# Weight loads queued three chunks further ahead in a mixture-of-experts stage

## The chip, the cores and the metric

The kernel runs on one core of a Trainium2 chip. The time is device microseconds of one execution, from a launch of the whole program; the median of three runs of the kernel before is 403.86 us (402.92 to 403.9). TensorE (PE) does the products, VectorE (DVE) and ScalarE (ACT) the elementwise work, GpSimd (POOL) some more and the indirect transfers, and SyncE's queue (SP) issues most of the others.

## The reference

A retention layer (attention without a softmax, with a decay mask) over 8 batches, 8 heads, 576 positions and 64 channels a head gives x, 4608 tokens of 512 channels. Then comes a mixture of 8 experts with one expert for each token, all in float32:

```python
skip_score = x @ w_skip
do_compute = skip_score > 0            # other tokens pass unchanged
xc = x[do_compute]
logits = xc @ w_gate
e_idx = np.argmax(logits, axis=1)      # one expert of 8 for each token
gate_w = softmax(logits)[e_idx]
for e in range(8):
    h = np.maximum(xc[mask] @ w1[e], 0.0)          # 512 -> 1024
    y[mask] = gate_w[mask, None] * (h @ w2[e])     # 1024 -> 512
out[do_compute] = xc + y
```

## The kernel before, in words

The first part (to about 155 us) computes the retention layer in 36 groups of 128 tokens, writes x to DRAM and sorts the tokens into lists, one for each expert. The experts are ranked by their number of tokens and run from the fullest to the emptiest; here they are counted in that order, 0 to 7. Expert e has room for `CAPS[e]` tokens (368, 344, 332, 308, 304, 286, 278, 276): two full blocks of 128 and a rest.

Float32 is reached with two operands of a shorter format: a value is split into hi, which ACT casts, and lo, the difference, which DVE subtracts. A product is then three: hi with hi, hi with lo, lo with hi (`three`). PE runs these in an order written out by hand.

The 1024 hidden channels of an expert go in 8 chunks of 128. A step of the loop in `experts` is one chunk f of one expert e: `up` multiplies the tokens (xhi, xlo) with the first weights of the chunk into ph, 12 products; ACT makes hhi of it and DVE hlo; and `down`, which runs one step later, multiplies these with the second weights, 12 products again. So PE's order is up of this chunk, down of the one before, up of the next.

The weights of a chunk are one transfer of 512 KB (`load_w`, L158) into a staging tile w, of which there are 4 buffers. The split (`split_w`, L166 to L168) makes whi on ACT and wlo on DVE, each with 6 buffers. At a step, `experts` loads all chunks up to `AHEAD` = 5 ahead of this one and splits what it has loaded. The split of a chunk waits for `down` of the chunk six before it, whose buffer it takes.

The tokens of expert e are gathered from DRAM during expert e-1 (`gather_next`). From expert 2 on they are turned without PE: the rows go to DRAM (`hop_out`, the tile hop), come back in four pieces of 32 partitions (`hop_in`, the tile xh), and DVE transposes them (`turn_pieces`, the tile xt) and they are split into xhi (ACT) and xlo (DVE). There is one such pass for each of the two full blocks, in steps 4 and 5 of the expert before, and in step 6 one for the rests (`turn_pack`). Rests of several experts share a block; only experts 2 and 4 fetch one of their own (hop r, xh r, xt r), experts 3, 5 and 6 take their columns of one that is there already, and so does expert 7.

What sets the order: PE's is by hand. For the other engines a scheduler lays the instructions out when the program is built, by its own idea of the times, and the engines then keep that order. `hop_out` and `hop_in` say that their transfers are to be issued after the load that was asked for last (`marks["load"]`).

Of the kernel before, what the change touches and what calls it, by code (L numbers as in the profile page):

```python
# [48 lines left out]
UAHEAD = UBUFS - LAG  # L49
VBUFS = 3  # L50
AHEAD = 5
GROUPS = (8, 8, 8, 4, 4, 4)
KONE = 2
QD = 32
# [5 lines left out]
NCUT = 5  # L60
# [23 lines left out]
def kernel(  # L84
# [70 lines left out]
    def load_w(e, f, regs):  # L155

        t = wpool.tile([P, 2, NCC, P], F32, tag="w", name=f"w_{e}_{f}", bufs=4)
        marks["load"] = nc.sync.dma_start(t.rearrange("p m c i -> p (m c i)"), w[bass.ds(regs[e], 1), f].rearrange("o p c -> (o p) c"))  # L158
        return t
# [281 lines left out]
    def blocks(e):  # L441
        return [(k, min(P, CAPS[e] - k * P)) for k in range(NBLK)]
# [34 lines left out]
    with ExitStack() as actx:  # L477
# [254 lines left out]

        starts = np.cumsum((0,) + GROUPS).tolist()
        todo = []
        counted = []
        added = []
        chunks = []

        def weights():
# [4 lines left out]
            chunks.append(None)  # L744
            if 0 <= n - 2 < AHEAD:
                t = chunks[n - 2]
                hi, lo = wq[0, n - 2] = parts(t)
                tc.keep_in_program_order(nc.scalar.copy(hi, t))
                behind = ranked[-1] if len(ranked) == len(GROUPS) - 1 else None
                for m in range(2):  # L750
                    for c in range(0, NCC, NCC // 2):
# [3 lines left out]
                        if behind is not None:  # L755
# [6 lines left out]
                            behind = None  # L762
            if n < AHEAD:
                chunks[n] = load_w(0, n, regs)
# [19 lines left out]
        def route(b):  # L784
# [3 lines left out]
            k = starts.index((b + 1) * NB) - 1  # L788
            ra = route_a(starts[k], GROUPS[k])
            more = lambda: route_b(ps_m, k == 0, k > KCUT, k == KRANK, *ra)  # L790
# [67 lines left out]
        if LAG:  # L858
            stage_c(NT - 2)
        while len(chunks) < AHEAD + 2:  # L860
            weights()
# [199 lines left out]
    def experts(acts):  # L1061


        every = blocks(0)
        early, late = every[: CUT // P], every[CUT // P :]
        steps = [(0, f, early) for f in range(NCUT)] + [None] + [(0, f, late) for f in range(NCUT)]
        steps += [(0, f, every) for f in range(NCUT, NFC)]
        steps += [(e, f, blocks(e)) for e in range(1, NE) for f in range(NFC)]
        chunks = [(e, f) for e in range(NE) for f in range(NFC)]
        xg = {0: xg0}  # L1070
        xT = {0: (xhi0, xlo0)}
        begun = range(len(hs))
        py = {}
        last = None

        between = {}
        raw = {}

        def split_raw(most):
            for c in list(raw)[:most]:  # L1080
                wq[c] = split_w(raw.pop(c))

        def behind(mark, do, *args):
            with tc.issue_after(marks[mark].ins):
                do(*args)

        def at(e, f, place, do, *args):
            between.setdefault((e, f, place), []).append(lambda: do(*args))

        def turn_next(e):  # L1090
            xT[e] = [mp.tile([P, NCC, CAP], F32R, tag=x, name=f"{x}_{e}") for x in ("xhi", "xlo")]
            if e > 1:
                for k in range(NBLK):
                    at(e - 1, 4 + k, 0, lambda k=k: behind("up", turn_block, e, k, *xT[e]))
                return
            for c in range(NCC):
                where = ((5, 0), (6, 0), (6, 1), (7, 0))[c]
                at(e - 1, *where, lambda c=c: turn(e, xg[e], *xT[e], blocks(e)[:-1], [c], ("pt", "m")[c % 2]))
                if c == 1:
                    at(e - 1, *where, lambda: turn_pack(e, *xT[e], "pt"))  # L1100

        at(2, 7, 1, count_more)
        at(0, 6, 0, pack_move)
        at(0, 7, 1, lambda: behind("up", pack_ids))
        at(NE - 1, 4, 0, lambda: tc.keep_in_program_order(nc.gpsimd.drain()))
        for e in range(2, NE):
            at(e - 1, 0, 0, lambda e=e: gather_next(e, xg))
            hops = [(f"{e}_{k}", lambda e=e, k=k: xg[e][:, k, :]) for k in range(NBLK - 1)]
            if e == PACKS[PLACE[e][0]][0]:
                hops.append((f"r{PLACE[e][0]}", lambda e=e: xr[PLACE[e][0]]))  # L1110
            for k, (name, rows) in enumerate(hops):
                at(e - 1, 2 + k // 2, k % 2, lambda name=name, rows=rows: hop_out(name, rows()))
                at(e - 1, 3 + k // 2, k % 2, lambda name=name: hop_in(name))
        for n in range(len(steps) + 1):
            cur = steps[n] if n < len(steps) else None
            if n in acts:
                acts[n]()
            if cur:
                e, f, ks = cur
                i = chunks.index((e, f))  # L1120
                for c in chunks[i : i + AHEAD + 1]:
                    if c not in wq and c not in raw and c[0] < len(regs):
                        raw[c] = load_w(*c, regs)
                if ks is not late and n > 3:
                    split_raw(1 if i == NCUT else len(raw))
                if (e, f) not in hs:
                    tg, nb = (f"_{f}", 1) if e == 0 and f < NCUT else ("", 3)
                    hs[e, f] = [
                        mp.tile([P, CAP], F32R, tag=f"{x}{tg}", name=f"{x}_{e}_{f}", bufs=nb) for x in ("hhi", "hlo")
                    ]  # L1130
                if n not in begun:
                    tag = ("ph", "ph", "m", "pt", "py3")[f] if ks is late else "ph"
                    ph = bank(tag, f"ph_{e}_{f}_{ks[0][0]}", 2 if tag == "ph" else 1)
                    if ks is late:
                        up_late(f, ph, ks, wq[e, f], hs[e, f])
                    else:
                        up(ph, ks, xT[e], wq[e, f], hs[e, f])
                if (n, 1) in acts:
                    acts[n, 1]()
                    behind("lists", split_raw, 1)  # L1140
                    gather_next(1, xg)
                if f == 3 and ks is not early and e + 1 < NE:
                    turn_next(e + 1)
            place = cur and cur[2] is not early and cur[:2]
            for do in between.pop((*place, 0), ()) if place else ():
                do()
            if last and last[2] is late and cur[2] is late:
                last = None
            if last and last[2] is late:
                for f in range(NCUT):  # L1150
                    down(0, f, late, py[0], hs[0, f], wq[0, f])
                split_raw(len(raw))
            elif last:
                e, f, ks = last
                if e not in py:
                    py[e] = [bank(f"py{c}", f"py_{e}_{c}") for c in range(NBLK if e == 0 else NCC)]
                if n == NCUT:
                    down(e, f, ks[:1], py[e], hs[e, f], wq[e, f])
                    for cs, tag in (((0, 1), "pt"), ((2, 3), "py3")):
                        turn(0, xg0, xhi0, xlo0, late, cs, tag)  # L1160
                    ks = ks[1:]
                down(e, f, ks, py[e], hs[e, f], wq[e, f])
                if f == NFC - 1:
                    y = evacuate(e, py[e])
                    if e + 1 < NE:
                        ks = blocks(e)[:-1] if e else blocks(e)
                        for k, where in zip(ks, ((1, 1), (2, 0), (2, 1))):
                            at(e + 1, *where, finish, e, y, xg[e], [k])
                        if e and PACKS[PLACE[e][0]][-1] == e:
                            at(e + 1, 2, 1, finish_pack, PLACE[e][0])  # L1170
                    else:
                        finish(e, y, xg[e], blocks(e)[:-1], ("pt", "m"))
                        k, n = blocks(e)[-1]
                        finish_rest(yR[e], n, xr[PLACE[e][0]], gate[:, k, e : e + 1], sidx[:, k, e : e + 1], "ph")
            for do in between.pop((*place, 1), ()) if place else ():
                do()
            last = cur
        assert not between
# [16 lines left out]
    with tc.For_i(0, nblock, 1):  # L1195
# [7 lines left out]
        reg = expert_reg(mei[0:1, 0:1])  # L1203
        ws = [split_w(load_w(0, f, [reg])) for f in range(AHEAD)]
        ps2 = bank("m", "ps2")
# [3 lines left out]
        raw = rt.tile([P, NCMP], F32, tag="raw2", name="raw2")  # L1209
# [17 lines left out]
        for f in range(NFC):  # L1227
            if f + AHEAD < NFC:
                ws.append(split_w(load_w(0, f + AHEAD, [reg])))
# [81 lines left out]
```

## Time and profile before

| | |
|---|---|
| median of three runs | 403.86 us |
| the profiled execution | 407.06 us |
| its span, first to last instruction | 405.4 us |
| PE, DVE, ACT, POOL busy | 380.5, 279.8, 184.0, 154.1 us |
| DMA, mean over the span | 245 GB/s |
| mean granted clock of PE | 0.992 |

The profile is of one execution. Its time is longer than that of the runs without a profile. Busy time of PE is modelled at the ends of products, so a PE that is busy all the time is one whose products start one behind the other. The experts' stage is the part from about 165 us to 397.

### The profile page before, as it was taken

How to read it: one execution, taken by the hardware profiler on the slowest of the kernel's cores; microseconds unless marked ns; L12 is line 12 of the kernel's file. 1: busy time of each engine (PE TensorE's matmuls, PEld its weight loads, DVE VectorE, ACT ScalarE, POOL GpSimd, SP SyncE). 2: the span in 40 equal slices, each digit the busy share in tenths (PEclk: the TensorE clock that was granted, in tenths of full speed). 3: DMA queues.
4: the chain of work that ended last, by engine and by line, in shares of the span. 5: the costliest groups of instructions: out<-in, count | busy, mean ns of one | idle time of the engine just before them, and what ended most of it. 6: DMA issues, size and time to landing. Idle time of an engine off the chain costs nothing. (4 is left out here: it accounts for less than half of the span.)

```text
span 405.4 us, 12478 instructions
## 1 busy us (share of the span) xinstructions
PE 380.5 (94%) x4950; PEld 345.4 (85%) x4952; DVE 279.8 (69%) x623; ACT 184.0 (45%) x367; POOL 154.1 (38%) x210
## 2 busy tenths in 40 slices
PE   7899989989999887999999999999999999999992
PEld 3677777778787775979899999999999999999992
DVE  3665686588589788977756766797768567777512
ACT  2454544445444566115544543545535546455311
POOL 4965654565475489051032024023042032200402
PEclk9999999999999899999999999999999999999998
DMA  8998999999999986236987666776776776673101
GB/s 304 352 331 306 352 303 350 321 335 308 331 348 325 352 327 185 81 86 224 311 261 251 202 203 212 235 254 233 244 218 238 227 243 226 233 259 107 66 2 56
DMA packets 39420, 99.34 MB, mean 245 GB/s; under 512 B 5678, under 2 KB 12974, under 8 KB 39358
## 3 DMA queue, kind: packets, MB, share of 16 engines
q1 hardware_dynamic: 30366, 78.66, 57.5%
q0 software_dynamic: 3232, 9.99, 7.2%
q10 hardware_dynamic: 5760, 9.85, 6.5%
q8 instruction: 40, 0.66, 0.7%
q14 instruction: 22, 0.18, 0.1%
HBM read 80.63 MB, written 18.26 MB: 244 GB/s over the span
## 5 line engine op out<-in xcount | busy, mean ns | idle before, releaser
L168 DVE TENSOR_TENSOR wlo_w<-w,whi_w 128x1024 fp32r<-128x1024 f32 x59 | 71.9, 1224 | 38.3 <-ACT whi_w L167 37.7
L167 ACT CAST whi_w<-w 128x1024 fp32r<-128x1024 f32 x59 | 61.7, 1051 | 52.2 <-PE py L449 48.6
L981 POOL DMA_INDIRECT out<-rs,sidx x17 | 21.5, 1264 | 126.3 <-DVE rs L980 118.1
L449 PE MATMUL ph<-xhi,whi_w 128*128 128x344 f32 (+6 forms) x224 | 68.4, 305 | 0.0
L449 PE MATMUL py<-hhi,whi_w 128*128 128x344 f32 (+6 forms) x224 | 68.2, 304 | 0.0
L449 PE MATMUL py<-hhi,wlo_w 128*128 128x344 f32 (+6 forms) x224 | 67.7, 302 | 0.0
L449 PE MATMUL ph<-xlo,whi_w 128*128 128x344 f32 (+6 forms) x224 | 67.7, 302 | 0.0
L449 PE MATMUL ph<-xhi,wlo_w 128*128 128x344 f32 (+6 forms) x224 | 67.7, 302 | 0.0
L449 PE MATMUL py<-hlo,whi_w 128*128 128x344 f32 (+6 forms) x224 | 67.6, 302 | 0.0
L588 POOL TENSOR_TENSOR kn<-u,tt_sb 128x512 f32<-128x512 f32 x33 | 35.0, 1060 | 46.6 <-DMA u<-qkv 19.4
L457 ACT ACTIVATE hhi<-ph 128x344 fp32r<-128x344 f32 (+8 forms) x61 | 26.0, 426 | 57.3 <-PE ph L449 57.2
L580 ACT COPY u<-psc 64x256 f32<-64x256 f32 x64 | 23.4, 366 | 58.5 <-DVE u L576 52.5
L670 PE MATMUL pxt<-u,vs 128*64 128x128 f32 (+1 forms) x576 | 49.0, 273 | 0.1
L607 POOL TENSOR_TENSOR vs<-u,tt_sb 64x256 f32<-64x256 f32 x72 | 44.8, 622 | 9.5 <-PE pxt L670 4.4
L576 DVE TENSOR_TENSOR u<-psc,mt_sb 64x256 f32<-64x256 f32 x72 | 30.3, 420 | 23.5 <-PE pxt L646 10.5
L621 PEld LDWEIGHTS ps_s<-u,kn 128*64 128x64 f32 x512 | 31.8, 139 | 12.8 <-issue 5.9
L449 PEld LDWEIGHTS ph<-xhi,whi_w 128*128 128x128 f32 x224 | 42.2, 189 | 0.1
L449 PEld LDWEIGHTS ph<-xlo,whi_w 128*128 128x128 f32 x224 | 42.2, 188 | 0.1
L449 PEld LDWEIGHTS py<-hhi,whi_w 128*128 128x128 f32 x224 | 42.2, 189 | 0.0
L449 PEld LDWEIGHTS py<-hlo,whi_w 128*128 128x128 f32 x224 | 42.2, 188 | 0.0
L449 PEld LDWEIGHTS py<-hhi,wlo_w 128*128 128x128 f32 x224 | 42.2, 188 | 0.0
L449 PEld LDWEIGHTS ph<-xhi,wlo_w 128*128 128x128 f32 x224 | 42.2, 188 | 0.0
(216 smaller groups left out, 825.0 us busy)
## 6 DMA issues: line engine op xcount, KB each, us to landing
u<-qkv SPq DMA_DIRECT2D x72, 512.0 KB, 5.9
w<-w SPq DMA_DIRECT2D x64, 512.0 KB, 4.6
out<-xn ACTq DMA_DIRECT2D x36, 256.0 KB, 5.9
hop<-xg SPq DMA_DIRECT2D x12, 256.0 KB, 4.7
xh<-hop SPq DMA_DIRECT2D x48, 64.0 KB, 2.7
hop_r<-xr SPq DMA_DIRECT2D x2, 256.0 KB, 2.7
xh_r<-hop_r SPq DMA_DIRECT2D x8, 64.0 KB, 5.0
out<-rs,sidx POOLq DMA_INDIRECT x17, 5.8
```

Source lines behind the costliest of these rows:

```text
L167: nc.scalar.copy(hi, t)
L168: nc.vector.tensor_tensor(lo, t, hi.bitcast(F32), ALU.subtract)
L449: nc.tensor.matmul(ps, x, y, start=first and n == 0, stop=last and n == 3 * len(terms) - 1)
L457: nc.scalar.activation(hi, ph, AF.Relu)
L576: nc.vector.tensor_tensor(u_t[g][h, j, :, :D], near[h, :, :D], mt_sb[h].unsqueeze(1).broadcast_to([D, NPR, D]), ALU.mult)
L580: nc.scalar.copy(u_t[g][h, j, :, D:], near[h, :, D:])
L588: nc.gpsimd.tensor_tensor(kn_t[g].rearrange("p a (j i) -> p a j i", j=2), u_t[g][:, 3].rearrange("p a (j i) -> p a j i", j=2), tt_sb[:, k ...
L607: nc.gpsimd.tensor_tensor(vs_t[g][h, j], u_t[g][h, 2, :, j * D : (j + 1) * D], tt_sb[h, TV + g % NQ // 2, :].unsqueeze(2).broadcast_to([D, ...
L621: nc.tensor.matmul(ps_s[halves[j], i % 2, a, :], kn_t[g][:, a, j * D : (j + 1) * D], u_t[g][:, 2, a, j * D : (j + 1) * D], start=i == 0 an ...
L670: nc.tensor.matmul(pxt[halves[j], a, q], vs_t[g][:, j, a, :], u_t[g][:, j, a, q], start=False, stop=a == NPR - 1, skip_group_check=True,)
L981: done = nc.gpsimd.indirect_dma_start(out=out, out_offset=bass.IndirectOffsetOnAxis(ap=idx, axis=0), in_=rs[:n], in_offset=None, bounds_ch ...
```

## The change

A constant `LEAD` = 3 is added. From expert 1 on, a step asks for the loads of chunks up to 8 ahead instead of 5. What it splits are still the chunks up to 5 ahead: the others stay loaded and unsplit until their turn. The four staging buffers stay.

```diff
 AHEAD = 5
+LEAD = 3
...
-                for c in chunks[i : i + AHEAD + 1]:
+                for c in chunks[i : i + AHEAD + 1 + (LEAD if e else 0)]:
                     if c not in wq and c not in raw and c[0] < len(regs):
                         raw[c] = load_w(*c, regs)
+                due = sum(c in chunks[: i + AHEAD + 1] for c in raw)
                 if ks is not late and n > 3:
-                    split_raw(1 if i == NCUT else len(raw))
+                    split_raw(1 if i == NCUT else due)
```

No instruction is added or taken away. PE and GpSimd keep their order; SP, DVE and ACT get another one. On SP, where expert 2's rows are sent to DRAM and back, the rows before are these (w_7 is chunk 7 of expert 1, w_0 and w_1 are chunks of expert 2):

```order
L158 DMA w_7_3802<-w 128x1024
L1016 DMA hop_0_3825<-xg_3738 128x512
L1016 DMA hop_1_3844<-xg_3738 128x512
L354 TENSOR_LOAD order
L158 ISA
L158 DMA w_0_3851<-w 128x1024
L1022 DMA xh_0_3876<-hop_0_3825 32x4x128 x4
L1016 DMA hop_r_3881<-xr_3745 128x512
L1022 DMA xh_1_3895<-hop_1_3844 32x4x128 x4
L158 ISA
L158 DMA w_1_3900<-w 128x1024
L1022 DMA xh_r_3923<-hop_r_3881 32x4x128 x4
```

And now (w_2, w_3 and w_4 are all of expert 2; every line number is one higher):

```order
L159 DMA w_2_3808<-w 128x1024
L1017 DMA hop_0_3831<-xg_3744 128x512
L1017 DMA hop_1_3850<-xg_3744 128x512
L159 ISA
L159 DMA w_3_3857<-w 128x1024
L1023 DMA xh_0_3882<-hop_0_3831 32x4x128 x4
L1017 DMA hop_r_3887<-xr_3751 128x512
L1023 DMA xh_1_3901<-hop_1_3850 32x4x128 x4
L159 ISA
L159 DMA w_4_3906<-w 128x1024
L1023 DMA xh_r_3929<-hop_r_3887 32x4x128 x4
```

The hops and what fetches them back stand three loads further back, the order among them being the same.

On DVE at the end of expert 1, where expert 2's tokens are transposed, before (hlo_5 to hlo_7 are of expert 1, wlo_w_2 to wlo_w_4, xt and xlo of expert 2):

```order
L458 SCALAR_TENSOR_TENSOR hlo_5_3951<-ph_5_0_3952,hhi_5_3950 128x344
L1026 STREAM_TRANSPOSE xt_1_3967<-xh_1_3895 128x4x4x32
L168 TENSOR_TENSOR wlo_w_2_3944_3947<-w_2_3944,whi_w_2_3944_3946 128x1024
L173 TENSOR_TENSOR xlo_3875<-xt_1_3967,xhi_3874 128x4x128
L458 SCALAR_TENSOR_TENSOR hlo_6_3990<-ph_6_0_3991,hhi_6_3989 128x344
L1026 STREAM_TRANSPOSE xt_r_4006<-xh_r_3923 128x4x4x32
L168 TENSOR_TENSOR wlo_w_3_3983_3986<-w_3_3983,whi_w_3_3983_3985 128x1024
L173 TENSOR_TENSOR xlo_3875<-xt_r_4006,xhi_3874 128x4x76
L458 SCALAR_TENSOR_TENSOR hlo_7_4029<-ph_7_0_4030,hhi_7_4028 128x344
L168 TENSOR_TENSOR wlo_w_4_4022_4025<-w_4_4022,whi_w_4_4022_4024 128x1024
```

And now:

```order
L1027 STREAM_TRANSPOSE xt_1_3973<-xh_1_3901 128x4x4x32
L459 SCALAR_TENSOR_TENSOR hlo_6_3996<-ph_6_0_3997,hhi_6_3995 128x344
L174 TENSOR_TENSOR xlo_3881<-xt_1_3973,xhi_3880 128x4x128
L169 TENSOR_TENSOR wlo_w_3_3857_3992<-w_3_3857,whi_w_3_3857_3991 128x1024
L459 SCALAR_TENSOR_TENSOR hlo_7_4035<-ph_7_0_4036,hhi_7_4034 128x344
L1027 STREAM_TRANSPOSE xt_r_4012<-xh_r_3929 128x4x4x32
L174 TENSOR_TENSOR xlo_3881<-xt_r_4012,xhi_3880 128x4x76
L169 TENSOR_TENSOR wlo_w_4_3906_4031<-w_4_3906,whi_w_4_3906_4030 128x1024
```

The transposes have moved back by one place or two; xt_r now stands behind hlo_7. ACT follows: its cast of xt_r (xhi) stands behind hhi_7.

On DVE at the end of expert 3, where expert 4's tokens are transposed, before:

```order
L458 SCALAR_TENSOR_TENSOR hlo_6_4748<-ph_6_0_4749,hhi_6_4747 128x308
L1026 STREAM_TRANSPOSE xt_r_4764<-xh_r_4681 128x4x4x32
L168 TENSOR_TENSOR wlo_w_3_4741_4744<-w_3_4741,whi_w_3_4741_4743 128x1024
L173 TENSOR_TENSOR xlo_4633<-xt_r_4764,xhi_4632 128x4x48
L458 SCALAR_TENSOR_TENSOR hlo_7_4787<-ph_7_0_4788,hhi_7_4786 128x308
L168 TENSOR_TENSOR wlo_w_4_4780_4783<-w_4_4780,whi_w_4_4780_4782 128x1024
L458 SCALAR_TENSOR_TENSOR hlo_0_4822<-ph_0_0_4823,hhi_0_4821 128x304
```

And now:

```order
L169 TENSOR_TENSOR wlo_w_3_4615_4750<-w_3_4615,whi_w_3_4615_4749 128x1024
L174 TENSOR_TENSOR xlo_4639<-xt_1_4731,xhi_4638 128x4x128
L459 SCALAR_TENSOR_TENSOR hlo_7_4793<-ph_7_0_4794,hhi_7_4792 128x308
L1027 STREAM_TRANSPOSE xt_r_4770<-xh_r_4687 128x4x4x32
L169 TENSOR_TENSOR wlo_w_4_4664_4789<-w_4_4664,whi_w_4_4664_4788 128x1024
L174 TENSOR_TENSOR xlo_4639<-xt_r_4770,xhi_4638 128x4x48
L459 SCALAR_TENSOR_TENSOR hlo_0_4828<-ph_0_0_4829,hhi_0_4827 128x304
```

Here the last xlo stands behind the split of chunk 4 (wlo_w_4); on ACT, too, its cast stands behind whi of chunk 4. Where expert 6 and expert 7 are prepared, the last xlo moves from in front of wlo of chunk 3 to behind it.

## Rows read from the trace of the kernel before

**Rows 1.** Busy us (instructions) by engine in the experts' stretch, granted clock, DMA, GB/s.

```profile
200.00:395.00 195.00, 195.00 (x1404) 194.41 (x1403) 132.46 (x209) 90.97 (x150) 40.82 (x31) 1.00 0.63 208
```

**Rows 2.** Timeline of POOL at the end: start, length, line, operation, idle before.

```profile
400.97 0.90 POOL L981 DMA_INDIRECT out<-rs_yR,sidx  x1 [0.30 <-issue]
```

**Rows 3.** Waits of SP's queue: who for whom, us in total, times, longest.

```profile
SPq L158 <- DVE wlo_w L168: 83.0, 36, 5.5
```

**Rows 4.** Timeline of SP, expert 2's transfers.

```profile
198.62 1.03 SPq L1016 DMA_DIRECT2D hop<-xg  x2
...
204.09 1.75 SPq L1022 DMA_DIRECT2D xh<-hop  x4
```

**Rows 5.** Timeline of DVE in expert 1 (split of chunk 6; last block).

```profile
208.61 1.23 DVE L168 TENSOR_TENSOR wlo_w<-w,whi_w 128x1024 fp32r<-128x1024 f32 x1 [1.83 <-ACT whi_w L167]
...
225.89 1.10 DVE L1026 STREAM_TRANSPOSE xt_r<-xh_r 128x512 f32<-128x512 f32 x1
...
228.64 0.47 DVE L173 TENSOR_TENSOR xlo<-xt_r,xhi 128x304 fp32r<-128x304 f32 x1
229.02 0.51 DVE L458 SCALAR_TENSOR_TENSOR hlo<-ph,hhi 128x344 fp32r<-128x344 f32 x1
```

**Rows 6.** The tile hop: its hops and the fetches from it.

```profile
L1016 SPq DMA_DIRECT2D hop<-xg x12: 367/378/878, 198.6 to 344.0; - x12
...
DMA to landing us min/median/max: 1.9/2.9/5.4
```

**Rows 7.** The tile xh_r: fetches of the block of rests.

```profile
L1022 SPq DMA_DIRECT2D xh_r<-hop_r x8: 376/431/463, 209.0 to 270.9; - x8
...
DMA to landing us min/median/max: 4.0/5.0/6.2
```

**Rows 8.** Timeline of DVE in expert 3.

```profile
267.28 0.15 DVE L905 CAST nmore<-ends 128x1 int32<-128x1 f32 x1
...
269.39 1.25 DVE L168 TENSOR_TENSOR wlo_w<-w,whi_w 128x1024 fp32r<-128x1024 f32 x1
...
287.87 0.35 DVE L173 TENSOR_TENSOR xlo<-xt_r,xhi 128x192 fp32r<-128x192 f32 x1
288.14 0.47 DVE L458 SCALAR_TENSOR_TENSOR hlo<-ph,hhi 128x308 fp32r<-128x308 f32 x1
290.11 1.23 DVE L168 TENSOR_TENSOR wlo_w<-w,whi_w 128x1024 fp32r<-128x1024 f32 x1 [1.50 <-ACT whi_w L167]
```

**Rows 9.** Timeline of ACT at the end of expert 1.

```profile
227.36 0.44 ACT L172 CAST xhi<-xt_r 128x304 fp32r<-128x304 f32 x1
228.51 0.46 ACT L457 ACTIVATE hhi<-ph 128x344 fp32r<-128x344 f32 x1 [0.71 <-PE ph L449]
```

**Rows 10.** Timeline of PE, expert 2's first product with xlo.

```profile
230.31 0.31 PE L449 MATMUL ph<-xlo,whi_w 128*128 128x332 f32 x1
```

**Rows 11.** Timeline of ACT at the end of expert 3.

```profile
286.60 0.35 ACT L172 CAST xhi<-xt_r 128x192 fp32r<-128x192 f32 x1
...
289.03 1.05 ACT L167 CAST whi_w<-w 128x1024 fp32r<-128x1024 f32 x1 [0.87 <-PE py L449]
```

**Rows 12.** Timeline of PE, expert 4's first product with xlo.

```profile
289.11 0.30 PE L449 MATMUL ph<-xlo,whi_w 128*128 128x304 f32 x1
```

**Rows 13.** Timeline of DVE at the ends of experts 5 and 6.

```profile
339.35 0.69 DVE L173 TENSOR_TENSOR xlo<-xt,xhi 128x512 fp32r<-128x512 f32 x1
...
341.38 1.23 DVE L168 TENSOR_TENSOR wlo_w<-w,whi_w 128x1024 fp32r<-128x1024 f32 x1 [0.81 <-ACT whi_w L167]
...
367.20 1.22 DVE L168 TENSOR_TENSOR wlo_w<-w,whi_w 128x1024 fp32r<-128x1024 f32 x1 [0.79 <-ACT whi_w L167]
```

**Rows 14.** Timeline of PE, first products with xlo of experts 6 and 7.

```profile
343.54 0.29 PE L449 MATMUL ph<-xlo,whi_w 128*128 128x278 f32 x1
...
369.25 0.29 PE L449 MATMUL ph<-xlo,whi_w 128*128 128x276 f32 x1
```

**Rows 15.** Busy us by engine in three stretches of the first part (columns as Rows 1).

```profile
136.00:139.65 3.65, 1.92 (x61) 1.53 (x59) 3.41 (x11) 1.68 (x5) 1.69 (x3) 1.00 0.97 355
139.65:143.06 3.41, 3.41 (x40) 3.02 (x36) 1.14 (x3) 2.48 (x6) 2.13 (x4) 0.50 1.03 412
...
150.00:153.00 3.00, 1.55 (x26) 1.15 (x24) 2.75 (x11) 0.26 (x2) 1.95 (x3) 1.00 0.53 181
```

## The prediction

> **What bounds the kernel now.** I read the busy time by stretch first, then who waits for whom, then the timelines of VectorE (DVE), ScalarE (ACT) and TensorE (PE) around the places where one expert ends and the next begins. From 200 to 395 us PE is busy for 195.00 of 195.00 us at the full granted clock [rows 1], and the view of PE's waits lists none in that stretch. So the experts' stage runs at the pace of its products. An edit there can't make it shorter by removing a wait, because PE has none; it can only add one. Whatever it adds reaches the end, since PE has no idle time in which to win it back, and the last rows of the output are only sent out after PE's last products: the last indirect DMA starts at 400.97 us [rows 2].
>
> Do the loads of weights limit anything? SyncE's queue (SP) waits 83.0 us in 36 pieces at L158, the load, for the DVE half of a split [rows 3]. That is the release of a staging buffer: there are four, so the load of a chunk waits until the chunk four before it is split. SP is thus already as far ahead as four buffers let it be.
>
> **The change part by part.** *The loads.* From expert 1 on (counted from 0, in the order in which they run) each step asks for chunks up to eight ahead instead of five. No instruction is added or removed on any engine, and the buffers stay four, so a load still starts when the split four chunks earlier is done. The loads themselves therefore don't move in time by more than the transfers that stand before them in the queue: I cost this at 0, and what hides it is that PE waits for no weights now and would not in the new order either.
>
> *The transfers of the tokens.* What does move is everything that SP issues between loads. An expert's rows go out to DRAM and back (hop, then xh) so that DVE can transpose them, and these transfers are queued behind the load that was issued last. That load is now three chunks later, so they are too: hop 0 and 1 stood behind chunk 7 of expert 1 and stand behind chunk 2 of expert 2. In the trace they were issued at 198.62 us and the first pieces fetched back at 204.09 [rows 4], and DVE transposes the last block at 225.89 [rows 5], 21.8 us after that fetch began. New time for expert 2: chunk 2's load waits for the split that ends at 208.61 + 1.23 = 209.84 [rows 5]; a hop landed in at most 5.4 us [rows 6], so xh 0 is issued by about 215.3; three times four pieces at 1.75 for four, with hop r and one load between them at up to 0.5 each [rows 4], end at 221.6, and the pieces of xh r landed within 6.2 us [rows 7]: 227.8. For expert 4 the same sum starts at 269.39 + 1.25 = 270.64 [rows 8] and ends with the issue at 282.4 and the landing at 286.4 to 288.6 (4.0 to 6.2). The data still come before their new turn on DVE (229.4 and 288.6, below), for expert 4 only just.
>
> *SP's other work.* Reading the number of left-over blocks (L1194) also changes its place in SP's queue, from between the loads of chunks 5 and 6 to between 1 and 2 of expert 4. What it reads is written at 267.28 [rows 8], before the load of chunk 2 could start (270.64), so 0.
>
> *The turn on DVE and ACT.* This is where it costs. The order on these two engines is fixed when the program is built, and the transposes now stand later in it. PE and GpSimd keep their order. For expert 2 the block of rests, xt r, moves from between hlo 6 and wlo 3 to behind hlo 7. hlo 7 can't come earlier than now: it needs hhi 7, which ACT makes when PE has finished the block ph, 228.51 + 0.46 = 228.97 [rows 9]. From there, with the durations of the present rows: hlo 7 to 229.53; transpose 1.10 (it overlaps its predecessor by 0.08) to 230.54; the cast xhi on ACT 0.44 and 0.03 to hand over, 231.01; the difference xlo 0.47, to 231.50 [rows 5, 9]. PE wants its first product with xlo at 230.31 [rows 10]. In the present order xlo is ready at 228.64 + 0.47 = 229.11, 1.2 us early; in the new one it is 231.50 - 230.31 = **1.2 us late**.
>
> For expert 4 the slip is larger, because the split of chunk 4 comes in between. In the new order xhi stands behind whi 4 on ACT and xlo behind wlo 4 on DVE. whi 4 waits for PE to leave the old chunk's buffer, which is exactly when PE turns to expert 4, and it runs 289.03 to 290.08 [rows 11]; wlo 4 follows to 290.11 + 1.23 = 291.34; xlo, 0.35 long with the usual overlap of 0.09, ends at 291.60 [rows 8]. The transpose before them (from 288.14 + 0.47 = 288.61 on, 1.10, so to 289.7) and the cast (0.35 behind whi 4, to 290.35) are hidden by that split. PE wants this xlo at 289.11 [rows 12]: 291.60 - 289.11 = **2.5 us late**. Now it is ready at 287.87 + 0.35 = 288.22.
>
> Experts 3, 5, 6 and 7 fetch no rest of their own. For 3 and 5 the last xlo stays ahead of chunk 3's split. For 6 and 7 it falls behind it: 341.38 + 1.23 = 342.61 at the earliest, 342.7 with the work now queued before it, plus 0.69 less the overlap, 343.3 against a use at 343.54; and for 7, 367.3 + 1.23 + 0.69 less the overlap, 369.1 to 369.2 against 369.25 [rows 13, 14]. Both just fit: 0, with an upper end of 0.4 together.
>
> *Sum.* 1.2 + 2.5 = 3.7 us. The profiled execution took 407.06 us (span 405.4), so it becomes 410.8. The median of the runs without that profile is 403.86, 3.2 us less; with the same 3.7 us added, **407.6 us**. Bounds: below, the chains could hand over faster or PE could take other operands first, which I bound at 1.5 us off the sum. Above, expert 4's xt r has 290.11 - 289.7 = 0.4 us before it pushes wlo 4 back; if it is a us late, by its rows or by DVE's work before it, 0.6 is added; and 0.4 for experts 6 and 7.
>
> **A clock that falls.** The granted clock fell once inside the work: PE was busy 1.92 of the 3.65 us to 139.65, and then ran 3.41 us at 0.50 of full speed, the lower of its two levels, 1.2 GHz. A stretch with PE busy 1.55 of 3.00 us, at 150, kept 1.00 [rows 15]. In expert 4's new stall PE would stand still for most of 2.5 us, which lies near both. A fall of that length costs half of 3.41, 1.7 us, and makes 409.3. The Trainium skill (TensorE: Matmul & The Clock Gate, "What's actually happening") has throttled as the default state, which activity lifts; by that rule a stall inside this dense stretch is charged twice, and the sum would be 5.4 instead of 3.7. The rows here show one fall and one stay, so they support it in part only, and I keep it as a rival.
>
> **The rivals.**
> - *The clock falls in expert 4's stall.* For: the row to 139.65. Against: the row at 150, and about 20 us of dense work on either side. 409.3 us.
> - *The rows land late.* Transfers issued close behind a 512 KB load take longer (up to 6.2 us for xh r, against a median of 2.9 for hop and xh) [rows 6, 7]. If xh 0 or xh r lands 1 to 3 us after its turn, DVE stands, and everything behind it (hlo, the next split) with it. For: the margin of expert 4 is near 0. Against: expert 2 has 1.6 us. It adds 0.5 to 2 us: 408.1 to 409.6.
> - *Only one of the two stalls shows*, because a handover is shorter than I think: 405.1 to 406.4.
> - *Not slower.* The present cover (1.2 us for expert 2, 288.22 to 289.11 = 0.9 for expert 4) would still do. That is decided at the end of xlo: before 230.31 and before 289.11. For: the scheduler's order keeps the same work per step, DVE has idle time (132.46 of 195 us busy), and the transfers no longer stand ahead of loads in SP's queue. Against: hlo 7 and whi 4 are both tied to PE's own progress, so idle time earlier on DVE doesn't help. There is no wait on PE to remove either, so its price is 0: 403.9.
>
> **How the numbers follow.** Forecast, both stalls at about their size: 0.60. Clock: 0.14. Late rows: 0.12. One stall: 0.06. Not slower: 0.08, of which 0.02 is for faster by over 0.3%. That much, 1.2 us, is about what a measurement of this kernel can tell from no change; slower than that begins at 405.1. Slower is 0.60 + 0.14 + 0.12 + 0.05 = 0.91, leaving 0.01 of the single stall at that edge; same is 0.06 + 0.01 = 0.07, faster 0.02. The sum's own bounds are 406.1 (less 1.5) and 408.6 (0.6 and 0.4 more). The range goes on to 405.3, for a single stall, and to 409.9, for one fall of the clock together with late rows.
>
> **What would show it.** In the profile after: PE idle at the first products of experts 2 and 4 (ph at L449's counterpart), put down to DVE's xlo, with about 1.2 and 2.5 us, and nowhere else between 200 and 395; hop issues about 11 us later against the products than now; loads of weights at the same distance from the splits. The forecast is wrong if PE shows no idle there, if the stalls belong to xh's landing instead of DVE's order, or if the clock is at 0.50 after expert 4's start.

## The result and the profile after

| | before | after |
|---|---|---|
| median of six runs beside each other | 403.67 us | 410.38 us |
| lowest of them | 402.92 us | 406.95 us |
| the profiled execution | 407.06 us | 411.15 us |
| its span | 405.4 us | 409.5 us |

The ratio is 1.0143 [1.0098, 1.0189]: 5.8 us slower, 4.0 to 7.6. One of the six runs of the changed kernel, 416.1 us, was in a slower state and is not in the ratio; the median of the other five is 409.62 us. That is just inside the range on record, whose upper end is 409.9 us (a ratio of 1.015), and the interval reaches beyond that end; the forecast's own 407.6 us is a ratio of 1.0093, just under the interval. The direction and the place were right; the sum is short by some 2 us. The profiled execution came near the 410.8 us forecast for it by luck: its first part happened to be 1.44 us shorter than the one in the profile before.

The experts' stage, first by stretch (columns as [rows 1]):

```profile
200.00:292.50 92.50, 89.56 (x592) 87.98 (x591) 65.82 (x109) 41.91 (x66) 18.54 (x16) 1.00 0.73 226
292.50:295.90 3.40, 3.40 (x16) 3.40 (x15) 0.83 (x3) 0.90 (x3) 0.00 (x0) 0.50 0.42 146
295.90:400.00 104.10, 104.10 (x797) 104.03 (x796) 66.06 (x100) 47.37 (x82) 18.83 (x14) 1.00 0.55 180
```

Two things are new against [rows 1]. PE is idle for 92.50 - 89.56 = 2.9 us before 292.5, and right behind that the granted clock is at its lower level for 3.40 us. The waits of PE between 200 and 395 us, where there were none (who for whom, us in total, times, longest):

```profile
PE ph L450 <- ACT xhi L173: 2.1, 2, 1.4
PE ph L450 <- DVE xlo L174: 0.7, 1, 0.7
```

PE's timeline at the first products of expert 2 and of expert 4 (start, length, engine, line, operation, out<-in; in brackets the idle time before and who ended it):

```profile
228.56 0.32 PE L450 MATMUL py<-hhi,wlo_w 128*128 128x344 f32 x1
229.61 0.42 PE L450 MATMUL ph<-xhi,whi_w 128*128 128x332 f32 x1 [0.73 <-ACT xhi L173]
230.12 0.42 PE L450 MATMUL ph<-xlo,whi_w 128*128 128x332 f32 x1
230.38 0.31 PE L450 MATMUL ph<-xhi,wlo_w 128*128 128x332 f32 x1
...
288.74 0.30 PE L450 MATMUL py<-hhi,wlo_w 128*128 128x308 f32 x1
290.42 0.41 PE L450 MATMUL ph<-xhi,whi_w 128*128 128x304 f32 x1 [1.38 <-ACT xhi L173]
291.57 0.41 PE L450 MATMUL ph<-xlo,whi_w 128*128 128x304 f32 x1 [0.74 <-DVE xlo L174]
291.81 0.30 PE L450 MATMUL ph<-xhi,wlo_w 128*128 128x304 f32 x1
...
292.37 0.34 PE L450 MATMUL ph<-xhi,whi_w 128*128 128x304 f32 x1
292.51 0.45 PE L450 MATMUL ph<-xlo,whi_w 128*128 128x304 f32 x1
292.75 0.46 PE L450 MATMUL ph<-xhi,wlo_w 128*128 128x304 f32 x1
```

Products normally start 0.16 us apart in expert 1, 0.15 in expert 2 and 0.14 in experts 3 and 4. A product's modelled length overlaps the next one, so what a stall costs is read from the starts, less this normal distance: 229.61 - 228.56 - 0.16 = 0.89 and 230.12 - 229.61 - 0.15 = 0.36, together **1.25 us** at expert 2; 290.42 - 288.74 - 0.14 = 1.54 and 291.57 - 290.42 - 0.14 = 1.01, together **2.55 us** at expert 4. Behind the product with xlo the next one starts 0.1 us later than normal at both places (230.38 and 291.81). From 292.5 on the starts are about 0.25 apart instead of 0.14: the clock. The waits list nothing more in experts 5 to 7.

DVE around both places:

```profile
226.25 1.23 DVE L169 TENSOR_TENSOR wlo_w<-w,whi_w 128x1024 fp32r<-128x1024 f32 x1 [0.26 <-ACT whi_w L168]
227.56 0.52 DVE L459 SCALAR_TENSOR_TENSOR hlo<-ph,hhi 128x344 fp32r<-128x344 f32 x1
228.00 1.08 DVE L1027 STREAM_TRANSPOSE xt_r<-xh_r 128x512 f32<-128x512 f32 x1
229.59 0.47 DVE L174 TENSOR_TENSOR xlo<-xt_r,xhi 128x304 fp32r<-128x304 f32 x1 [0.51 <-ACT xhi L173]
...
288.38 0.47 DVE L459 SCALAR_TENSOR_TENSOR hlo<-ph,hhi 128x308 fp32r<-128x308 f32 x1
288.87 1.11 DVE L1027 STREAM_TRANSPOSE xt_r<-xh_r 128x512 f32<-128x512 f32 x1
290.02 1.23 DVE L169 TENSOR_TENSOR wlo_w<-w,whi_w 128x1024 fp32r<-128x1024 f32 x1
291.16 0.35 DVE L174 TENSOR_TENSOR xlo<-xt_r,xhi 128x192 fp32r<-128x192 f32 x1
```

and ACT:

```profile
229.11 0.45 ACT L173 CAST xhi<-xt_r 128x304 fp32r<-128x304 f32 x1 [1.58 <-DVE xt_r L1027]
...
288.94 1.04 ACT L168 CAST whi_w<-w 128x1024 fp32r<-128x1024 f32 x1 [1.05 <-PE py L450]
290.01 0.55 ACT L173 CAST xhi<-xt_r 128x192 fp32r<-128x192 f32 x2
```

They answer to [rows 5, 8, 9, 11]: xt_r stands behind hlo of chunk 7, and at expert 4 the split of chunk 4 stands between it and the last xlo. The handovers on DVE and ACT that the prediction walked through are here. SP's queue at both places, against [rows 4]; measured from expert 1's first product (198.29 us here, 199.73 before) the hops are issued 11.6 us later than they were, about 11 forecast:

```profile
208.79 0.95 SPq L1017 DMA_DIRECT2D hop<-xg  x2
...
213.55 1.75 SPq L1023 DMA_DIRECT2D xh<-hop  x4
...
219.98 1.80 SPq L1023 DMA_DIRECT2D xh_r<-hop_r  x4
...
271.03 0.88 SPq L1017 DMA_DIRECT2D hop<-xg  x2
...
280.99 1.85 SPq L1023 DMA_DIRECT2D xh_r<-hop_r  x4
```

and the waits of that queue (whole span, then 200 to 400 us):

```profile
SPq L159 <- DVE wlo_w L169: 86.0, 34, 7.1
...
SPq L1023 <- DMA w<-w: 7.1, 5, 2.6
```

The loads still spend 86.0 us waiting for a split to free a buffer, 83.0 before [rows 3]. New is that the fetches xh are listed as waiting for loads to land, 7.1 us in five waits. The prediction's sum of the transfers had no such term: the last fetch for expert 2 is issued by 219.98 + 1.80 = 221.78, where the forecast's 221.6 is 220.2 in this profile's time, where expert 1 begins 1.44 us earlier.

### The profile page after: what moved, and what is told of

Read it like the earlier page. It is cut to its first block, busy times and chain, and to the rows that moved or that the text cites. A ratio compares the mean times of both kernels' runs of the same rounds, so it can differ in the third digit from the quotient of the medians.

```text
span 409.5 us, 12478 instructions
## 1 busy us (share of the span) xinstructions
PE 381.3 (93%) x4952; PEld 345.3 (84%) x4952; DVE 282.9 (69%) x623; ACT 183.6 (45%) x367; POOL 151.8 (37%) x210
## 5 line engine op out<-in xcount | busy, mean ns | idle before, releaser
L671 PE MATMUL pxt<-u,vs 128*64 128x128 f32 (+1 forms) x576 | 47.8, 269 | 1.5 <-issue 1.5
```

What stands on the lines that cost most here:

```text
L671: nc.tensor.matmul(pxt[halves[j], a, q], vs_t[g][:, j, a, :], u_t[g][:, j, a, q], start=False, stop=a == NPR - 1, skip_group_check=True,)
```

## The experiments

All ran beside the kernel before, the first four on one chip, the other four on a second one. "Stage" is the time from expert 1's first product to the last product of expert 7, read from PE's timeline: 196.7 us before, 202.4 after, 5.7 more. The medians contain besides a first part whose length varies from one execution to the next: expert 1 began at 199.73 us in the profile before, at 198.29 after, and between 196.49 and 198.51 in the eight below. So the stalls are read from the profiles, and the ratios say whether they reach the end.

The rival theories: **order** (the transposes' place on DVE and ACT makes the stalls), **landing** (the rows arrive too late, because their transfers stand three loads further back), and for the missing 2 us **clock**.

**The changed kernel again.**

> The changed kernel once more, for comparison on one chip. Theory (order on DVE and ACT): PE idle 1.2 us at the first products of expert 2 and 2.5 us at those of expert 4, 3.8 together, and in those executions in which the granted clock falls behind the second stall 1.5 us more: 407.5 to 409.5, about +0.9 to +1.5% on the kernel before. Rival (no clock part): +0.9% in every run.

411.0 us, 1.015 [1.0101, 1.0199]. Stalls of 1.45 and 2.54 us; the clock at 0.50 behind the second, from 292.25 on. The two stalls and the fall are no accident of one execution.

**Products in the gaps.** Products of 128x512 that nobody reads are put ahead of the first product of expert 2 and of expert 4.

```diff
+FILL = {2: 6, 4: 12}
...
+                        if f == 0 and e in FILL:
+                            pf = bank("m", f"fill_{e}")
+                            for _ in range(FILL[e]):
+                                nc.tensor.matmul(pf, warm[:, :P], warm, start=True, stop=True)
                         up(ph, ks, xT[e], wq[e, f], hs[e, f])
```

> The changed kernel, with 6 products of 128x512 (bf16, into a bank that nobody reads) put on PE in front of expert 2's first product and 12 in front of expert 4's: PE waits just as long, but works. Theory (the stall costs its own length, and a fall of the clock on top of it): the clock stays at 1.00 behind 289 us, the products take 18 x 0.21 = 3.8 us, and the time is 407.5, below the changed kernel by up to 1.5 us and with less spread. Rival (the clock's fall has nothing to do with the stall): the clock falls as before, and the time is that of the changed kernel or, where the products don't fit the stalls, above it.

409.93 us, 1.0147 [1.0108, 1.0186]. PE's timeline at expert 4, and the whole stage by stretch:

```profile
287.78 0.30 PE L451 MATMUL py<-hhi,wlo_w 128*128 128x308 f32 x1
287.93 2.76 PE L1143 MATMUL fill<-mc 128*128 128x512 bf16 x12
290.34 0.49 PE L451 MATMUL ph<-xhi,whi_w 128*128 128x304 f32 x1
290.94 0.41 PE L451 MATMUL ph<-xlo,whi_w 128*128 128x304 f32 x1
```

```profile
200.00:400.00 200.00, 199.68 (x1427) 195.87 (x1426) 132.57 (x211) 90.60 (x154) 36.59 (x30) 1.00 0.63 200
```

The clock kept 1.00 throughout in this profile: the fall goes with PE standing still, and is not tied to the place. The expected time was missed, because the operands came later. Expert 4's first product starts 2.56 us behind the last one instead of 1.68, which is as long as the filling lasts, but the second gap shrank to 0.46 us in return (290.34 to 290.94, less 0.14), and the end of both gaps is set by xlo, which is later here because its transpose waits for the rows:

```profile
288.34 1.18 DVE L1028 STREAM_TRANSPOSE xt_r<-xh_r 128x512 f32<-128x512 f32 x1 [0.44 <-DMA xh_r<-hop_r]
...
290.49 0.40 DVE L175 TENSOR_TENSOR xlo<-xt_r,xhi 128x192 fp32r<-128x192 f32 x1
```

At expert 2 the first product starts 1.49 us behind the last one instead of 1.05, when xhi is ready; DVE came to xt_r 0.4 us later against PE. In all the gaps cost 4.6 us here instead of 3.8, and the stage is 5.0 us longer than before instead of 5.7, without a fall. The medians, with their intervals of 3 us, can't tell this kernel from the changed one; only the profile separates the two.

**The old turn, the new queue.** Loads and transfers as in the changed kernel, but on DVE and ACT the transposes and casts of the rests for experts 2 and 4 are held at their old places by explicit order edges (those of step 6 are shown). The full blocks keep the later places of the changed kernel.

```diff
+                    if f == 6 and q is not None:
+                        behind("up", lambda: xrT.update({q: turn_pieces(f"r{q}")}))
+                        with tc.issue_after(marks["turn"].ins):
+                            split_raw(due)
```

> The changed kernel with its loads and transfers in the new places, but with the transpose and split of the rests of experts 2 and 4 held on DVE and ACT where the kernel before has them: the transpose ahead of wlo of chunk 3, the split ahead of hlo of chunk 7. Theory (order): no idle of PE at 230 and 289 us, 403.7, no difference to before within 0.3%. Rival (the rows themselves come too late since their transfers stand three loads further back): DVE waits for the landing instead, PE is idle at the same places, and the time stays at 407 to 410.

409.35 us, 1.0128 [1.0092, 1.0164]. At expert 2 the stall is gone: its products follow each other without a gap. At expert 4 it stays, 1.72 and 0.86, in all 2.58 us, and the clock falls at 290.49. DVE's timeline there:

```profile
285.88 0.69 DVE L174 TENSOR_TENSOR xlo<-xt,xhi 128x512 fp32r<-128x512 f32 x1 [0.83 <-ACT xhi L173]
287.81 1.08 DVE L1027 STREAM_TRANSPOSE xt_r<-xh_r 128x512 f32<-128x512 f32 x1 [1.23 <-DMA xh_r<-hop_r]
288.81 1.19 DVE L169 TENSOR_TENSOR wlo_w<-w,whi_w 128x1024 fp32r<-128x1024 f32 x1
289.91 0.36 DVE L174 TENSOR_TENSOR xlo<-xt_r,xhi 128x192 fp32r<-128x192 f32 x1
```

Now the idle time ahead of the transpose is ended by a transfer: the rests' rows land 1.23 us after DVE is free for them. In both profiles of the changed kernel the same transpose waits for nothing, because its new place is no earlier than the landing; with the gaps filled it waited 0.44 us even there. The place of the full blocks does not make the stall here, since DVE is free before the rows are there. At expert 4, order (by the next run) and landing (by this one) are each enough by themselves; at expert 2 it is the order alone.

**The new turn, the old queue.** The kernel before; only the turn of the rests for experts 2 and 4 is one step later, behind hlo of chunk 7, and for expert 4 the cast and the difference behind the split of chunk 4.

```diff
-                    at(e - 1, 4 + k, 0, lambda k=k: behind("up", turn_block, e, k, *xT[e]))
+                    put_off = k == NBLK - 1 and e in (2, 4)
+                    at(e - 1, 4 + k + put_off, 0, lambda k=k, do=turn_rests if put_off else turn_block: behind("up", do, e, k, *xT[e]))
```

Not shown is `turn_rests`, which does the turn and holds the cast and the difference of expert 4 behind that split.

> The kernel before, its loads and its queue untouched, with only the transpose and split of the rests of experts 2 and 4 moved on DVE and ACT to where the changed kernel has them. Theory (order): PE idle 1.2 us at expert 2 and 2.5 us at expert 4, and the time of the changed kernel, 407.5 to 409.5. Rival (what costs is in SP's queue): no idle, 403.7.

408.72 us, 1.0111 [1.0066, 1.0156]. PE's waits between 200 and 395 us (L1057 and L1059 are the cast and the difference that this kernel writes separately for expert 4):

```profile
PE ph L449 <- ACT xhi L1057: 1.2, 1, 1.2
PE ph L449 <- DVE xlo L1059: 0.9, 1, 0.9
PE ph L449 <- ACT xhi L172: 0.7, 1, 0.7
```

Both stalls, 1.25 and 2.55 us, and the fall, at 291.22, with no load or transfer moved; the stage is 5.5 us longer. The order alone is enough for 5.5 of the 5.7 us.

**The lead in one expert alone**, during expert 1 (which prepares expert 2) or during expert 3.

```diff
-                for c in chunks[i : i + AHEAD + 1 + (LEAD if e else 0)]:
+                for c in chunks[i : i + AHEAD + 1 + (LEAD if e == 1 else 0)]:
```

> The lead of three chunks in the steps of expert 1 alone, so that only the preparation of expert 2 is moved. Theory: one stall of 1.25 us at expert 2's first products, none at expert 4, and no fall of the clock behind it, since PE stands still for less than 1 us at a time: +1.25, 405.3. Rival (any stall takes the clock down): +1.25 and 1.5 to 1.6 more in the profile, 406.9.

> The lead of three chunks in the steps of expert 3 alone, so that only the preparation of expert 4 is moved. Theory: one stall of 2.55 us at expert 4's first products, and in most executions a fall of the clock to 0.50 behind it, 1.5 to 1.6 us more: 406.6 to 408.2. Rival (the fall needs both stalls): 406.6 at 1.00.

Expert 1 alone: 406.22 us, 1.0032 [1.0006, 1.0057], or 1.3 us (0.2 to 2.3). One stall, at expert 2, of 1.68 us, a little more than in the changed kernel, since DVE comes to xt_r 0.4 us later against PE. Expert 3 alone: 408.29 us, 1.0086 [1.0054, 1.0117], or 3.5 us (2.2 to 4.7). One stall, at expert 4, of 2.54 us. By stretch, first expert 1 alone, then expert 3 alone:

```profile
200.00:395.00 195.00, 193.76 (x1396) 192.81 (x1395) 131.22 (x209) 90.00 (x150) 39.67 (x30) 1.00 0.65 205
```

```profile
288.33:291.74 3.41, 3.33 (x13) 3.33 (x14) 0.03 (x1) 0.07 (x1) 0.00 (x0) 0.50 0.85 279
```

The short stall leaves the clock at 1.00; the long one is followed by 3.41 us at 0.50. Expert 3's lead costs more than twice what expert 1's does.

**A lead of two.** The scheduler lays out DVE and ACT exactly as in the kernel before, while the transfers stand two loads further back.

```diff
-LEAD = 3
+LEAD = 2
```

> The changed kernel with LEAD = 2. DVE and ACT then keep the order of the kernel before, word for word; on SP the tokens' transfers stand two loads further back. Theory (a stall comes where a block's turn on DVE, or its landing, passes the use): no turn has moved, and the landing of expert 4's rests, which with LEAD = 3 ended 2.35 us behind its turn of before (287.8 against 285.46), comes a chunk (3.4 us) earlier: no stall, 404.0, within 0.3% of before. Rival (each chunk of lead costs its share): two thirds of 3.8, 406.5, with PE idle at experts 2 and 4.

404.24 us, 0.9988 [0.9961, 1.0015], and no wait of ph. The tile xh_r there (landings min/median/max):

```profile
L1027 DVE STREAM_TRANSPOSE xt_r<-xh_r x2: 1099/1100/1100, 223.1 to 282.6; 128x512 f32<-128x512 f32 x2
...
DMA to landing us min/median/max: 4.6/7.0/7.1
```

The view mixes two blocks: the pieces for expert 2 landed in 7.0 to 7.1 us and those for expert 4 in 4.6. Transfers that stand two loads further back are still covered, even so, and loads asked for two chunks earlier gain nothing. For expert 4 the cover is small: the last piece is issued at 277.5 and lands at about 282.1, for a turn at 282.6. With the third load both covers go: the scheduler's order changes, and expert 4's rows land after their old turn, as the run with the old turn shows.

**The lead with the transfers at their old load.** Loads are asked for three further ahead, but what the hops are held behind stays the load five chunks ahead.

```diff
+        loads = {}
...
                         raw[c] = load_w(*c, regs)
+                        loads[c] = marks["load"]
+                marks["load"] = loads.get(chunks[min(i + AHEAD, len(chunks) - 1)], marks["load"])
```

> The loads are asked for three chunks further ahead as in the changed kernel, but the tokens' transfers are still held behind the load that they stood behind before. DVE, ACT, PE and GpSimd keep the order of the kernel before. Theory (the loads by themselves do nothing, their buffers hold them where they are): 403.9, no stall. Rival (something in the loads' own place costs, beside the two stalls): up to 1 us more than before.

404.62 us, 0.9994 [0.9962, 1.0026]. The stage by stretch, which reads like [rows 1]:

```profile
200.00:395.00 195.00, 195.00 (x1406) 194.41 (x1405) 132.69 (x210) 90.61 (x152) 38.07 (x30) 1.00 0.66 206
```

The stage is 196.7 us, as before. So the loads' lead itself is worth nothing in either direction (up to some 0.3%, the interval). The hops are issued where they were (197.34 us, 1.2 before expert 1's first product; 1.1 in the kernel before), and DVE and ACT keep the order of the kernel before; but loads now stand between the pieces of the fetches, and the last piece of xh_r for expert 2 is issued by 19.2 us after that product instead of 11.2. This slip is covered. All of the loss comes through what is tied to the load asked for last. No version here is faster than the kernel before.

## Why the prediction was right, and where it was short

*The bound, the loads, the direction: right.* PE had no idle time in which to hide a wait [rows 1], four buffers kept the loads where they were, and the kernel with the transfers at their old load shows the loads' part at 0.

*The turn: right, and nearly to the digit.* With the new positions, expert 2's chain was to end at 231.50, when PE's wish was at 230.31 [rows 10]; in the profile after, expert 1 begins 1.44 us earlier, which makes 230.06, and xlo ends at 229.59 + 0.47 = 230.06. At expert 4, 291.60 against 289.11 [rows 12] was forecast; PE is 0.09 earlier there, and xlo ends at 291.16 + 0.35 = 291.51. Stalls of 1.2 and 2.5 us were forecast, 1.25 and 2.55 measured. The profile puts the larger part down to ACT's xhi instead of DVE's xlo, because the product with xhi comes first and hangs on the same transpose. That splits the stall in two and does not change its sum. Experts 6 and 7, of which the forecast said that both just fit, 0 to 0.4 us: 0.08 and 0.09 us longer in the profile after, and 0.28 at expert 7 with the gaps filled.

*"The data still come before their new turn, for expert 4 only just": right in both profiles of the changed kernel, 0.44 us too late with the gaps filled, and it hid a second cause.* Landing was forecast at 286.4 to 288.6 for a turn at 288.6. The question that was not asked is how the landing stands against the *old* turn, in the trace before:

```profile
285.46 1.10 DVE L1026 STREAM_TRANSPOSE xt_r<-xh_r 128x512 f32<-128x512 f32 x1
```

By the forecast's own numbers the rows land 0.9 to 3.1 us after 285.46. With the old turn held they were late indeed, and cost the same 2.6 us as the order does. So the late rows, one of the rivals, added nothing in the two profiles of the changed kernel, but only because the order was as late as they were. It is the reason why restoring the order alone wins back only expert 2's part.

*The step that failed is the sum, which stopped at the two stalls.* After the second, the clock is at its lower level for 3.4 us. Expert 4 takes 30.72 us on PE from its first product to expert 5's, 28.07 before; 1.01 of the difference is the gap in front of xlo, which leaves 1.64. With the gaps filled and the clock up, the same reckoning (28.64, a gap of 0.46) leaves 0.11, so the fall itself is **1.5 us**. The prediction had this as a rival at 1.7 us with a chance of 0.14, and the clock at 0.50 after expert 4's start was one of its own signs of being wrong. That the measured time lies inside the range all the same is owed to the room at its upper end, which was meant for a fall together with late rows. With the fall the sum is 1.25 + 2.55 + 1.5 = 5.3; with 0.2 for the two products that start late behind xlo, and 0.17 in experts 6 and 7, it is the 5.7 by which the stage grew. The Trainium skill (TensorE: Matmul & The Clock Gate, "What's actually happening") has throttled as the default state, which activity lifts; that rule was weighed there and came to 5.4. The trace agrees with it at expert 4, where the stall was charged twice; at expert 2 the clock stayed at 1.00. The error was in weighing the rows: of [rows 15], a stretch with PE busy 1.55 of 3.00 us that kept its clock was set against one with 1.92 of 3.65 that lost it, and the dense work on either side was counted as a protection. It gave none here. The stretch of the new stall, in the profile after, and the smaller one at expert 2:

```profile
288.90:292.50 3.60, 1.48 (x9) 1.12 (x8) 2.57 (x3) 1.59 (x3) 0.00 (x0) 1.00 0.66 240
228.70:230.20 1.50, 0.68 (x4) 0.27 (x2) 0.85 (x2) 1.09 (x2) 0.00 (x0) 1.00 0.76 289
```

The one at expert 4 lost its clock right afterwards, and so did the same stretch in every profile with that stall left idle (the changed kernel twice, old turn with new queue, new turn with old queue, expert 3 alone). After the stall at expert 2, 1.25 to 1.68 us in four profiles, the clock stayed, as it did where products filled the gaps.

So one term is missing, what a stall costs after it is over: three fifths of the stall itself. Why the stretch at 150 us kept its clock with as little work is not settled. The distance by the ratio, 5.8 us, and the 5.7 of the stage agree within the interval. The spread of a few us in the first part stays unexplained; no run here was made for it.

## What to carry to other kernels

When one queue carries both bulk loads and small transfers that are held behind "the load asked for last", asking earlier for loads does not start them earlier if a buffer's release bounds them; it moves the small transfers back, and with them, through the scheduler, the work of engines that the change doesn't name. Read the new order on every engine, follow each moved instruction to the product that needs it, and ask for both the data's arrival and the turn, each against the old and the new deadline. Where PE is dense, price a new stall like the one of 2.55 us as the stall and a fall of the clock behind it.

## What the runs showed of the hardware

- A stall of 2.54 to 2.58 us, with one product in its middle, in a stage that had run at the full clock for some 90 us, was answered by some 3.4 us at 0.50 in five profiles of five, which began between 0.1 us before the stall's end and 1.3 us after it; a stall of 1.25 to 1.68 us in none of four. In the one profile with products that nobody reads in the gaps, the clock stayed at 1.00.
- The fetches of 64 KB from DRAM are listed as waiting 7.1 us in all for loads of 512 KB on the same queue to land, a wait that the trace before does not list. In the other three profiles with the whole lead and the transfers behind it these waits are 5.5, 6.1 and 9.8 us; with the old queue, a lead of two, or the lead in one expert, at most 1.4.
- The landing of the rests' rows is not ordered by their place in the queue. For expert 2 it took a median of 6.1 us before, 7.0 with a lead of two and 3.8 in the changed kernel; for expert 4, 4.1 before and 4.6 with a lead of two, and the changed kernel's trace has none on record.
